# First tokens loaded ahead of the modulation weights, low parts of h fused, and one pair of heads loaded later: an adaLN transformer block on one core

## Chip, cores, metric

One Trainium2 chip, one NeuronCore. The metric is the device time of one execution in microseconds, median over runs. The engines are named as in the profile: PE (TensorE, with PEld for its weight loads), DVE (VectorE), ACT (ScalarE), POOL (GpSimd) and SP (SyncE, which in this kernel issues all the DMAs of before).

## What is computed

All is float32, with S = 2048 tokens, D = 512, 32 heads of 16, and a hidden width of 1792:

```
mod = silu(c) @ w_mod                    # 6 vectors of 512: sa, ca, ga, sb, cb, gb
h = layernorm(x) * (1 + ca) + sa
x = x + ga * (softmax_attention(h @ wqkv) @ wo)
h = layernorm(x) * (1 + cb) + sb
out = x + gb * (mish(h @ w1 + b1) @ w2)
```

## The kernel before

Matmuls get their precision from splitting: each operand is rounded to fp32r ("hi", suffix `_h`, `wh`, `qh`) and the rest is kept as a second fp32r tensor ("lo", `_l`, `wl`, `ql`). A product is three matmuls, hi·hi, hi·lo and lo·hi (`mm3`). `hi_copy` makes the first (L94 on ACT, L96 on DVE, L98 on POOL), `lo_sub` the second (L101).

The schedule is manual: every engine executes its instructions in the order in which the program emits them. The program has three stages.

1. **The prologue.** It loads x in 16 tiles of 128 tokens (`load_x`), the first two modulation vectors' weights (`wma`, 1 MB each) and slices of wqkv (`slice_load`), normalises the tokens and writes h and its low part, transposed, for four blocks of 512 tokens (`tb` 0 to 3). Per block: statistics on DVE and a few small POOL instructions (`stats_tb`), the normalisation in place on ACT (`apply_tb`, L385), transposes on PE into PSUM (L427 for the first block, L435 after), then `tr_tb`: ACT writes h_h (L440), DVE writes the unrounded value hf (L441), and DVE or POOL subtracts to give h_l (`LOV` names the k that DVE takes; L101). The first k and q products (L132 on `ring`) go in two parts: those that need only h_h early, those that need h_l late. Before that come the modulation vectors: 8 matmuls against `wma` (L449), two ACT copies (L453), 8 small matmuls that turn rows into columns (L455), and two DVE writes into `modc` (L463, L464); h_h needs both vectors. silu(c) is one ACT instruction and three of DVE (L361 to L364), on c loaded as a column of 512 single elements.
2. **The main loop.** `step(t)` for t from -20 to 511. It computes the row maxima of the scores (L553 and L539 with DVE reductions L555 and L541), the scores (L588), exponentials on ACT (L591), the products with v (L606), and beside them all remaining projections and the MLP as queued units. Hooks `at(h, f)` run f at half step h, so a step t has the hooks 2t and 2t+1; this is how every DMA of the loop gets its place in SP's queue. Heads are worked in pairs: `load_pair(pp)` is two loads of q rows (L313) and two of k rows (L322). Pair 3 is first read at t = 4, so at h = 8.
3. **The tail**, the MLP of the last block.

In SP's queue around the start of the loop: `load_pair(2)` at h = -22, `load_pair(3)` at -8, the four stores of the first maxima into q (`qa<-mt`, L577) at -6, `load_v(0)` (`vg`, L526) at -3, then the later modulation weights (`wm`, L700, by `mod_load`).

`free_banks` goes through the program at the end and drops the dependencies between two instructions of different engines on the ring of PSUM banks if they touch different banks and share no other tensor that one of them writes.

Of the kernel before, what the change touches and what calls it, by code (L numbers as in the profile page):

```python
# [18 lines left out]
def adaln_block(ctx: ExitStack, tc: tile.TileContext, x, wqkv, wo, w1, b1, w2, c, w_mod, out):  # L19
# [21 lines left out]
    LOV = ((1,), (), (1, 3), (1, 3))  # L41
# [10 lines left out]
    nc.scalar.preload_act_table_set("natural_log_exp_and_others")  # L52
# [22 lines left out]
    sel = cst.tile([P, 1], F32, name="sel")  # L75
    nc.gpsimd.memset(sel, 0.0)
    for k in range(DK):
        nc.gpsimd.memset(sel[32 * k:32 * k + 1, :], 1.0)
# [89 lines left out]
    def free_banks():  # L168
# [3 lines left out]
        for i in nc.cur_bb.bb.instructions:  # L172
            banks, names, made = set(), set(), set()
            for a in (*i.outs, *i.ins):
                v = getattr(a, "bass_ap", None)
                if v is not None and v.tensor.name != ring_t.tensor.name:
                    names.add(v.tensor.name)
                    if any(a is w for w in i.outs):
                        made.add(v.tensor.name)
# [149 lines left out]
    with ExitStack() as es:  # L329
        lp = es.enter_context(tc.tile_pool(name="lp", bufs=1))  # L330
        cc = lp.tile([P, DK], F32, name="cc")
        nc.sync.dma_start(cc, c.rearrange("o (k p) -> p (o k)", p=P))
# [7 lines left out]
        wma = [lp.tile([P, DK, D], F32, name=f"wma{i}") for i in range(2)]  # L340
# [13 lines left out]
        nc.gpsimd.memset(zer, 0.0)  # L354
        for i in range(NR):
            nc.gpsimd.memset(qa[i].bitcast(F32), 0.0)
        for i in range(2):
            nc.gpsimd.memset(ka[i].bitcast(F32), 1.0)

        e = lp.tile([P, DK], F32, name="sil_e")  # L360
# [3 lines left out]
        nc.vector.tensor_mul(sil, cc, e)  # L364

# [21 lines left out]
        def first_norm():  # L387

            mv = lp.tile([P, 4, 2], F32, tag="ln_mv4", name="ln_mv4", bufs=2)
            rs = lp.tile([P, 4, 4], F32, tag="ln_rs4", name="ln_rs4", bufs=3)  # L390
            for h in range(2):
                two = slice(2 * h, 2 * h + 2)
                for i in range(2 * h, 2 * h + 2):
                    st_ = lp.tile([P, 6], F32, tag="ln_st", name="ln_st", bufs=4)
                    nc.vector.bn_stats(out=st_, in_=xts[i])
                    nc.vector.bn_aggr(out=mv[:, i, :], in_=st_)
                nc.gpsimd.tensor_scalar(rs[:, 0, two], mv[:, two, 1], 1.0, EPS, op0=ALU.mult, op1=ALU.add)
                nc.gpsimd.tensor_scalar(rs[:, 3, two], mv[:, two, 0], -1.0, 0.0, op0=ALU.mult, op1=ALU.add)
                nc.gpsimd.tensor_tensor(rs[:, 1, two], rs[:, 0, two], nhalf.to_broadcast([P, 2]), op=ALU.pow)
                nc.gpsimd.tensor_mul(rs[:, 2, two], rs[:, 3, two], rs[:, 1, two])  # L400
                if h == 0:
                    hi_k = split_hi(1, 0)
            return rs, hi_k

        def split_hi(kind, i, eng="p"):
# [4 lines left out]
        def split_lo(kind, i, hi):  # L410
            lo = lp.tile([P, DK, P], F32R, tag="wl", name="wl", bufs=2)
            lo_sub("p", lo, slices[kind, i], hi)
            slices[kind, i] = (hi, lo)

        def first_apply(rs, i, eng):
            xt = xts[i]
            if eng == "a":
                nc.scalar.activation(xt, xt, AF.Identity, scale=rs[:, 1, i:i + 1], bias=rs[:, 2, i:i + 1])
            else:
                nc.vector.tensor_scalar(xt, xt, rs[:, 1, i:i + 1], rs[:, 2, i:i + 1], op0=ALU.mult, op1=ALU.add)  # L420

        def first_tr():
            pts = [bank(("ring", "ms", "ring", "acc")[k]) for k in range(DK)]
            for ii in ((0,), (1,), (2, 3)):
                for k in range(DK):
                    for i in ii:
                        nc.tensor.transpose(pts[k][:, i * P:(i + 1) * P], xts[i][:, k * P:(k + 1) * P], ident)  # L427
            return pts

        def tr_tb(tb, ks=range(DK), pts=None):  # L430
            for k in ks:
# [9 lines left out]
                nc.vector.tensor_scalar(hf, pt, modc[:, 1, k:k + 1], modc[:, 0, k:k + 1], op0=ALU.mult, op1=ALU.add)  # L441
                lo_sub("v" if k in LOV[tb] else "p", h_l[:, k, s], hf, h_h[:, k, s])

        rs, hi_k = first_norm()
        pr, pm = [], bank()[:, :2 * DK].rearrange("p (i k) -> p i k", k=DK)
        for i in range(2):
            pr.append(ring())
            for k in range(DK):
                nc.tensor.matmul(pr[i][32 * k:32 * k + 32, :], sil[:, k:k + 1].to_broadcast([P, 32]), wma[i][:, k, :],  # L449
                                 start=True, stop=True)  # L450
        for i in range(2):
            row = lp.tile([P, D], F32, tag="hf", name="row", bufs=6)
            nc.scalar.copy(row, pr[i])  # L453
            for k in range(DK):
# [1095 lines left out]
```

## Time and profile before

| | us |
|---|---|
| median of 3 runs | 1692.54 (1691.68 to 1693.66) |
| the profiled execution, its own time | 1691.02 |
| its span | 1689.2 |
| granted TensorE clock | 1.00 |

The profile page gives busy time by engine, the span in 40 slices, the DMA queues, the chain of work that ended last, and the costliest groups. The timeline gives instructions in order of time: start, duration, engine, line, operation, output<-inputs, shapes, count, and in brackets the idle time before and what ended it. Successive instructions of a line are merged (x4). "SPq" is SP issuing a DMA; its duration is that of the issue, not of the transfer. In the windows view the columns are PE, PEld, DVE, ACT and POOL busy us with counts, the granted clock, the busy share of the DMA engines and GB/s.

### The profile page before, as it was taken

What the parts mean: (1) busy time and instruction counts of PE and PEld (TensorE: products, weight loads), DVE (VectorE), ACT (ScalarE), POOL (GpSimd) and SP (SyncE); (2) the same over time, 40 slices, a digit from 0 to 9 for tenths busy, and PEclk for the clock granted to TensorE, in tenths of its full rate; (3) what the DMA queues carried; (4) which work ended last, traced back from release to release, by engine and by line L of the source; (5) the groups of instructions that cost most, each with busy time, mean ns of one, the idle gap of its engine ahead of it and who ended that gap; (6) DMA issues with size and microseconds to landing.
All of it is one profiled execution on the core that took longest, in us unless ns stands there. A gap on an engine that the chain in (4) does not pass through costs nothing.

```text
span 1689.2 us, 33772 instructions
## 1 busy us (share of the span) xinstructions
PE 1667.3 (99%) x12418; PEld 921.5 (55%) x12418; DVE 1441.5 (85%) x2369; ACT 1355.1 (80%) x2612; POOL 821.1 (49%) x843
## 2 busy tenths in 40 slices
PE   7999999999999999999999999999999999999999
PEld 5755655555444455555555455555555455555687
DVE  8898888888989988888889888888889888883377
ACT  6257777777778998888888998888888998889674
POOL 7555224655313564556323564556323565555442
PEclk9999999999999999999999999999999999999999
DMA  7877556777755443434355434534354533533261
GB/s 248 269 244 199 147 150 185 218 223 216 231 142 146 110 94 98 117 88 129 84 137 152 115 77 93 139 77 127 87 144 122 130 94 77 144 107 132 75 230 63
DMA packets 115406, 238.98 MB, mean 141 GB/s; under 512 B 24928, under 2 KB 50544, under 8 KB 109288
## 3 DMA queue, kind: packets, MB, share of 16 engines
q1 hardware_dynamic: 115240, 236.82, 49.9%
q8 instruction: 98, 1.61, 0.4%
q14 instruction: 68, 0.56, 0.1%
HBM read 180.48 MB, written 51.45 MB: 137 GB/s over the span
## 4 chain that ended last, share of the span: by engine, by line
PE 91%; DVE 3%; ACT 3%; DMA 2%; POOL 1%; issue 1%; SPq 0%; ACTq 0%; DVEq 0%; POOLq 0%
PE bk L606 29%; PE ring L588 22%; PE ring L539 20%; PE bk L139 11%; PE bk L132 3%; PE ring L1219 2%; PE ring L132 2%; DVE mx L541 2%; ACT pr L591 1%; PE ring L553 0%; DMA qa<-mt 0%; DMA xt<-in_A_x 0%; PE ring L922 0%; DMA kscr<-qh 0%; PE ring L568 0%
## 5 line engine op out<-in xcount | busy, mean ns | idle before, releaser
L541 DVE TENSOR_REDUCE mx<-ring 128x1 f32<-128x512 f32 x1968 | 1223.1, 682 | 150.0 <-PE ring L539 136.4
L591 ACT ACTIVATE pr<-ring 128x512 f32<-128x512 f32 x2048 | 1078.4, 603 | 207.1 <-PE bk L139 124.7
L539 PE MATMUL ring<-ka,qa 64*128 64x512 f32 x1968 | 817.9, 429 | 1.4 <-ACT pr L591 1.1
L588 PE MATMUL ring<-qa,ka 64*128 64x512 f32 x2048 | 759.1, 402 | 3.4 <-ACT pr L591 1.9
L606 PE MATMUL bk<-pr,vg 128*32 128x512 f32 x4096 | 545.1, 604 | 0.0
L539 PEld LDWEIGHTS ring<-ka,qa 64*128 64x128 f32 x1968 | 350.5, 184 | 326.2 <-DVE mx L541 251.3
L588 PEld LDWEIGHTS ring<-qa,ka 64*128 64x128 f32 x2048 | 373.7, 184 | 194.7 <-DVE mx L541 111.4
L139 PE MATMUL bk<-h,w 64*128 64x512 f32 (+1 forms) x1080 | 278.1, 390 | 0.0
L139 PE MATMUL bk<-w,a_h 64*128 64x512 f32 x632 | 210.9, 413 | 0.0
L139 PEld LDWEIGHTS bk<-h,w 64*128 64x128 f32 x1080 | 178.5, 184 | 9.3 <-ACT pr L591 1.5
L606 PEld LDWEIGHTS bk<-pr,vg 128*32 128x32 f32 x4096 | 81.2, 108 | 135.4 <-issue 126.0
L139 PE MATMUL bk<-w,a_l 64*128 64x512 f32 x316 | 124.0, 392 | 0.0
L139 PEld LDWEIGHTS bk<-w,a_h 64*128 64x128 f32 x632 | 106.8, 184 | 4.3 <-ACT hb L800 1.0
L978 POOL TENSOR_TENSOR y<-yd,y 128x512 f32<-128x512 f32 x44 | 56.9, 1293 | 89.0 <-ACT yd L977 79.7
L812 POOL TENSOR_SCALAR qq<-ee 128x512 f32<-128x512 f32 x25 | 15.5, 619 | 169.6 <-ACT ee L806 169.6
L828 POOL TENSOR_TENSOR qq<-qq,rr 128x512 f32<-128x512 f32 x42 | 54.1, 1289 | 85.9 <-ACT rr L822 85.9
L814 POOL TENSOR_TENSOR hb<-hb,ee 128x512 f32<-128x512 f32 x42 | 54.1, 1288 | 79.6 <-DVE ee L810 77.7
L139 PE MATMUL bk<-w,o_hl 64*128 64x512 f32 x288 | 79.1, 405 | 0.0
L101 POOL TENSOR_TENSOR a_l<-hb,a_h 128x512 fp32r<-128x512 f32 x53 | 73.1, 1379 | 4.4
L98 POOL TENSOR_SCALAR qh<-qf 128x512 fp32r<-128x512 f32 x27 | 16.7, 619 | 90.8 <-ACT qf L262 69.4
L139 PEld LDWEIGHTS bk<-w,a_l 64*128 64x128 f32 x316 | 58.3, 185 | 3.4
L139 PE MATMUL bk<-h_h,wl 64*128 64x512 f32 x168 | 57.2, 420 | 0.2 <-ACT pr L591 0.2
(219 smaller groups left out, 1909.1 us busy)
## 6 DMA issues: line engine op xcount, KB each, us to landing
ka<-kscr SPq DMA_DIRECT2D x124, 384.0 KB
w<-w2scr SPq DMA_DIRECT2D x56, 512.0 KB
w<-w1scr SPq DMA_DIRECT2D x46, 512.0 KB
vg<-vscr SPq DMA_DIRECT2D x32, 552.0 KB
qa<-qscr SPq DMA_DIRECT2D x124, 100.0 KB
kscr<-qh SPq DMA_DIRECT2D x16, 512.0 KB
qscr<-qh SPq DMA_DIRECT2D x32, 256.0 KB
w2scr<-hl SPq DMA_DIRECT2D x14, 512.0 KB
```

The costliest lines, as they stand in the source:

```text
L101: (nc.gpsimd if eng == "p" else nc.vector).tensor_sub(lo, src, hi.bitcast(F32))
L132: nc.tensor.matmul(acc, l, r, start=start, stop=stop)
L139: i = nc.tensor.matmul(acc, l[64 * g:64 * g + 64], r[64 * g:64 * g + 64], start=start and not then, stop=bool(stop and then))
L539: nc.tensor.matmul(pm, qt[64 * s:64 * s + 64, qs * P:(qs + 1) * P], kt[64 * s:64 * s + 64, kb * TB:(kb + 1) * TB], start=True, stop=True)
L541: nc.vector.tensor_reduce(out=mxs[n][:, s, 4 * j + qs, kb:kb + 1], in_=pm, op=ALU.max, axis=AX.X)
L588: nc.tensor.matmul(p_, kt[64 * s:64 * s + 64, kc * P:(kc + 1) * P], qt[64 * s:64 * s + 64, :], start=True, stop=True)
L591: e = nc.scalar.activation(pr, p_, AF.Exp, scale=SCALE)
L606: nc.tensor.matmul(accs[n][32 * h:32 * h + 32, :], vgs[n][:, o:o + 32], pts.pop((t, h)), start=(kc == 0), stop=(kc == 15))
L814: (nc.vector if tail else nc.gpsimd).tensor_mul(hb, hb, ee)
L828: nc.gpsimd.tensor_mul(qq, qq, rr)
L978: nc.gpsimd.tensor_add(y[i], yd, y[i])
L1219: nc.tensor.matmul(po[i // 2][:, i % 2, :], l[:, s], w[:, r, :], start=(f == 0 and j == 0), stop=(f == FT - 1 and j == 2))
```

## The change

It touches the prologue and one hook.

- c comes as a row of four runs of 512 bytes, on ACT's DMA queue, ahead of ACT's table load, and a PE transpose makes it a column.
- The loads go x 0 to 3, `wma` 0 in four parts, the first k slice, `wma` 1 in four parts, the first q slice, and the rest as before.
- PE transposes the identity into a spare bank, 8 times before c's transpose, 26 times after it and 4 times after the modulation (`keep_busy`).
- The fills of `ka` move from POOL to ACT copies, those of `qa` 3 and 4 and of `zer` behind POOL's first normalisation; the `sel` tile is gone.
- Each modulation vector is 16 matmuls of 128 columns, in the order of the loads, with a DVE copy, a PE transpose and a DVE write into `modc`.
- Statistics of tokens 0 to 1023 go by pairs of tiles (`stats_two`). Those of tiles 4 to 7 now stand on DVE behind the write of the second vector and ahead of the first block's hf.
- In `tr_tb`, hf becomes pt·scale - h_h in one DVE instruction, and h_l = hf + shift: a DVE add with a pointer scalar for the k in `LOV`, else a POOL add with a broadcast column. `LOV[0]` is (2, 3) instead of (1,).
- The split of the first v slice comes between the normalisations of tiles 5 and 6, so on DVE ahead of the third block's statistics instead of behind them.
- `free_banks` tells the blocks of h_h apart.
- `load_pair(3)` is at h = -2 instead of -8.

```diff
-    LOV = ((1,), (), (1, 3), (1, 3))
+    LOV = ((2, 3), (), (1, 3), (1, 3))
...
-        cc = lp.tile([P, DK], F32, name="cc")
-        nc.sync.dma_start(cc, c.rearrange("o (k p) -> p (o k)", p=P))
+        crow = lp.tile([DK, P], F32, name="crow")
+        nc.scalar.dma_start(crow, c.rearrange("o (k p) -> (o k) p", p=P))
+        nc.scalar.preload_act_table_set("natural_log_exp_and_others")
...
-        for i in range(2):
-            nc.sync.dma_start(wma[i], w_mod[:, i * D:(i + 1) * D].rearrange("(k p) m -> p k m", p=P))
+        def load_mod(i):
+            for k in range(DK):
+                nc.sync.dma_start(wma[i][k], w_mod[k * P:(k + 1) * P, i * D:(i + 1) * D])
         for t in range(4):
             load_x(t)
+        load_mod(0)
         slice_load(1, 0, lp, lp)
+        load_mod(1)
         slice_load(0, 0, lp, lp)
...
+        keep_busy(8)
+        cc = ring()[:, :DK]
+        nc.tensor.transpose(cc, crow, ident[:DK, :DK])
+        keep_busy(26)
...
+        hi_copy("a", ka[0], ones.to_broadcast([P, S]))
...
+        def mod_sums(i, ks):
+            for k in ks:
+                for m in range(DK):
+                    nc.tensor.matmul(prs[i][32 * m:32 * m + 32, :P], sil[:, k:k + 1].to_broadcast([P, 32]),
+                                     wma[i][k][:, m * P:(m + 1) * P], start=(k == 0), stop=(k == DK - 1))
+        def mod_cols(i):
+            row = lp.tile([P, P], F32, name=f"row{i}")
+            nc.vector.tensor_copy(row, prs[i][:, :P])
+            nc.tensor.transpose(prs[i][:, P:2 * P], row, ident)
+            cols = prs[i][:, P:2 * P:32]
...
-                nc.vector.tensor_scalar(hf, pt, modc[:, 1, k:k + 1], modc[:, 0, k:k + 1], op0=ALU.mult, op1=ALU.add)
-                lo_sub("v" if k in LOV[tb] else "p", h_l[:, k, s], hf, h_h[:, k, s])
+                nc.vector.scalar_tensor_tensor(hf, pt, modc[:, 1, k:k + 1], h_h[:, k, s].bitcast(F32), op0=ALU.mult,
+                                               op1=ALU.subtract)
+                if k in LOV[tb]:
+                    nc.vector.tensor_scalar_add(h_l[:, k, s], hf, modc[:, 0, k:k + 1])
+                else:
+                    nc.gpsimd.tensor_add(h_l[:, k, s], hf, modc[:, 0, k:k + 1].to_broadcast([P, TB]))
...
+        for q in range(2):
+            stats_two(q)
+        first_apply(3, "p")
+        for t in (*(t.bitcast(F32) for t in qa[3:]), zer):
+            nc.gpsimd.memset(t, 0.0)
+        mod_sums(0, (0, 1))
+        first_apply(0)
+        first_tr(0)
+        mod_sums(0, (2,))
+        first_apply(1)
+        first_tr(1)
+        mod_sums(0, (3,))
+        first_apply(2)
+        first_tr(2)
+        first_tr(3)
+        mod_cols(0)
+        hi_k = split_hi(1, 0, "a")
+        hi_copy("a", ka[1], ones.to_broadcast([P, S]))
+        split_lo(1, 0, hi_k, "v")
+        mod_sums(1, range(DK))
+        mod_cols(1)
+        keep_busy(4)
+        hi_q = split_hi(0, 0, "p")
+        split_lo(0, 0, hi_q, "p")
+        for q in range(2, 4):
+            stats_two(q)
+        tr_tb(0, pts=pts)
+        for i in range(4, 8):
+            first_apply(i)
+            if i == 5:
+                slice_split(2, 0, eng="v")
...
             if tb + 2 < NB:
                 stats_tb(tb + 2)
-            if tb == 0:
-                slice_split(2, 0, eng="v")
...
-    for pp, h in ((2, -22), (3, -8)):
+    for pp, h in ((2, -22), (3, -2)):
         at(h, lambda pp=pp: load_pair(pp))
```

More of the change, by code (lines that the diff above doesn't have):

```diff
@@ L176, in free_banks @@
                 if v is not None and v.tensor.name != ring_t.tensor.name:
[L177 removed]
+                    part = v.offset % (DK * S) // TB if v.tensor.name == h_h.tensor.name else 0
+                    names.add((v.tensor.name, part))
                     if any(a is w for w in i.outs):
[L179 removed]
+                        made.add((v.tensor.name, part))
                 elif v is not None:
@@ L451, in adaln_block @@
[L451 to L454, printed above, removed]
-                nc.tensor.matmul(pm[:, i, k:k + 1], row[:, k * P:(k + 1) * P], sel, start=True, stop=True)
-        for i in range(2):
-            first_apply(rs, i, "a")
-        split_lo(1, 0, hi_k)
-        hi_q = split_hi(0, 0, "a")
-        split_lo(0, 0, hi_q)
-        first_apply(rs, 2, "a")
-        first_apply(rs, 3, "v")
```

88 lines of the change are left out of this document (35 added, 53 removed).

## The prediction

> **What bounds the kernel now.** I read the page first, for what the end hangs on.
>
> ```profile
> span 1689.2 us, 33772 instructions
> PE 1667.3 (99%) x12418; PEld 921.5 (55%) x12418; DVE 1441.5 (85%) x2369; ACT 1355.1 (80%) x2612; POOL 821.1 (49%) x843
> PE 91%; DVE 3%; ACT 3%; DMA 2%; POOL 1%; issue 1%; SPq 0%; ACTq 0%; DVEq 0%; POOLq 0%
> ```
>
> PE is 91% of the chain; the other engines' shares must lie where PE isn't yet, or not always, the limit. The change alters only the prologue and one hook, so I read the chain of waits over the first 125 us next.
>
> ```profile
> 15.12 1.48 DVE xt L420
> ...
> 51.07 1.86 PE bk L132 x14
> ...
> 92.58 7.33 DMA kscr<-qh
> ```
>
> Ahead of 51 us the chain goes through DVE, POOL, ACT and a DMA as often as through PE (the first row is a DVE step of the first block). Behind 51 us it is PE nearly without a break, so what the prologue gains the end should gain too. Two views price the prologue: the windows, for the DMA rate, and the timeline.
>
> ```profile
> 0.00:5.00 5.00, 0.00 (x0) 0.00 (x0) 1.88 (x3) 1.49 (x2) 4.17 (x24) 1.00 0.51 140
> 5.00:10.00 5.00, 0.79 (x4) 0.20 (x8) 4.29 (x4) 0.00 (x0) 3.72 (x3) 1.00 1.05 408
> 10.00:15.00 5.00, 5.00 (x27) 2.62 (x19) 2.95 (x8) 2.67 (x5) 3.01 (x9) 1.00 1.08 387
> 15.00:20.00 5.00, 4.79 (x24) 4.47 (x23) 4.75 (x12) 2.07 (x4) 2.72 (x3) 1.00 1.06 400
> ```
>
> ```profile
> 0.72 0.44 SPq L332 DMA_DIRECT2D cc<-in_c  x1
> 3.17 0.20 ACT L361 ACTIVATE sil_e<-cc 128x4 f32<-128x4 f32 x1 [1.18 <-DMA cc<-in_c]
> 9.21 3.64 PE L449 MATMUL ring<-wma,sil 128*32 128x512 f32 x16 [9.21 <-DVE sil L364]
> 9.79 0.69 DVE L395 BATCH_NORM_STATS2 ln_st<-xt 128x6 f32<-128x512 f32 x1 [0.64 <-DMA xt<-in_A_x]
> 16.52 0.15 DVE L463 TENSOR_SCALAR modc<-bk 128x4 f32<-128x4 f32 x1
> 16.66 0.68 DVE L374 BATCH_NORM_STATS2 ln_st<-xt 128x6 f32<-128x512 f32 x1
> 18.18 0.42 PE L427 MATMUL bk<-ident,xt 128*128 128x128 f32 x1
> 18.39 0.64 PE L427 MATMUL ring<-ident,xt 128*128 128x128 f32 x2
> 19.07 0.78 ACT L440 ACTIVATE h_h<-ring,modc 128x512 fp32r<-128x512 f32 x1 [2.93 <-PE ring L427]
> 19.88 0.81 DVE L441 TENSOR_SCALAR hf<-ring,modc 128x512 f32<-128x512 f32 x1
> ```
>
> The DMA engines are full from 5 to 20 us, and x stands in their queue behind 2.1 MB of modulation weights. The first h_h comes at 19.07, after PE's transposes; the modulation was ready at about 16.7. DVE goes from four tiles' statistics at 16.66 straight into hf at 19.88: 3.2 us for four tiles. The rest of the prologue:
>
> ```profile
> 23.50 0.68 DVE L374 BATCH_NORM_STATS2 ln_st<-xt 128x6 f32<-128x512 f32 x1
> 25.74 2.08 PE L132 MATMUL ring<-h_l,wh 128*128 128x512 f32 x8
> 26.70 1.21 DVE L101 TENSOR_TENSOR wl<-wr,wh 128x1024 fp32r<-128x1024 f32 x1
> 29.43 5.06 POOL L101 TENSOR_TENSOR h_l<-hf,h_h 128x512 fp32r<-128x512 f32 x4
> 29.68 2.93 ACT L385 ACTIVATE xt<-xt,ln_rs 128x512 f32<-128x512 f32 x4
> 34.00 0.60 PE L435 MATMUL ring<-ident,xt 128*128 128x128 f32 x4
> 34.79 1.18 PE L132 MATMUL ring<-h_l,wh 128*128 128x512 f32 x4
> 35.28 0.19 POOL L376 TENSOR_SCALAR ln_rs<-ln_mv 128x4 f32<-128x4 f32 x1 [0.79 <-DVE ln_mv L375]
> 36.79 0.20 POOL L379 TENSOR_TENSOR ln_rs<-ln_rs 128x4 f32<-128x4 f32 x1
> 43.92 0.81 DVE L441 TENSOR_SCALAR hf<-ring,modc 128x512 f32<-128x512 f32 x1 [1.91 <-ACT h_h L440]
> 45.48 1.16 DVE L101 TENSOR_TENSOR h_l<-hf,h_h 128x512 fp32r<-128x512 f32 x1
> 49.36 1.05 PE L132 MATMUL ring<-h_l,wh 128*128 128x512 f32 x2 [1.03 <-POOL h_l L101]
> ```
>
> PE has little slack, but neither have DVE and POOL: the second block's h_l is ready at 29.43 + 5.06 = 34.5, and PE reads its fourth part at about 34.79 + 3 x 0.23 = 35.5. Before 49.36 PE waits outright for h_l, 1.03 us.
>
> **The loads.** The windows give the bytes moved: 0.70 MB by 5 us, 2.74 by 10, 4.67 by 15. The first x tile ends at 2.36 MB (two weight blocks of 1.05 MB and 0.26 MB), so at 9.1; DVE, which waited for it, sees it at 9.79, a lag of 0.7. In the new order x 0 to 3 end at 1.05 MB, the second vector's weights at 3.41, tile 7 at 4.72 as before. With c off SP everything starts about 0.4 earlier (L332). So the last part of the second vector lands at 11.7 - 0.4 + 0.7 = 12.0 and tile 7 at 15.1 - 0.4 + 0.7 = 15.4. Six more issues on SP hide behind a full queue; uncovered they would cost SP about 0.5 each.
>
> **The modulation.** The 16 products of 128 columns of one vector are as many columns as its four products of 512 (3.64 us for both vectors), so 0.45 for the part that lands last. Then a DVE copy of 128 columns (estimate 0.3, under half of L441's 512), a transpose (0.42), the write (0.15) and three handovers (0.15 together, estimate): modc is ready at 13.5. By then, if PE's transposes aren't late (a rival below), the tokens are transposed, and h_h starts there instead of at 19.07. The ACT copies that fill ka (at most four times L440's 0.78) and the POOL fills lie under the wait for weights. The POOL fills and `sel` removed from the start, the freed L362 and the old row-to-column matmuls gain nothing by themselves: the landing sets the time.
>
> **DVE's chain.** It now runs: modc, statistics of tiles 4 to 7 (13.5 + 3.2 = 16.7; tile 7 at 15.4 + 0.8 doesn't bind), the first block's hf and adds, the v split, the third block's statistics. The fused hf waits for h_h; that costs nothing, since at 43.92 the old hf already started when ACT's h_h ended. Its own price is not shown. From 19.88 to 23.50 lie four old hf and one subtraction, so 0.72 each; L441's 0.81 is the upper end, a two-operand pass of 512 columns the lower (0.65, by 26.70's 1.21 for 1024). I keep 0.72. The adds that end h_l are priced from these groups by form:
>
> ```profile
> L704 POOL TENSOR_TENSOR wm<-wm,sil 128x1024 f32<-128x1024 f32 x8 | 15.1, 1893 | 15.9 <-DMA wm<-in_w_mod 8.9 <-PE bk L139 5.7 <-PE bk L606 1.2
> L96 DVE CAST a_h<-hb 128x512 fp32r<-128x512 f32 x3 | 1.3, 428 | 0.3
> ```
>
> L704 has a broadcast operand as the new POOL add has, and takes 1.89 for 1024 columns; half of that is 0.95, and with a fixed part (estimate 0.1) 1.04 for 512, against 1.27 for the old subtraction (5.06 for four). Ends: 0.95 and 1.27. A DVE add with a pointer scalar stands between the one-operand cast (0.43) and L420's 1.48, which ran beside POOL. I take 0.9: nearest to the old subtraction beside POOL (1.16), less the 0.25 or so by which the cast is shorter than a two-operand pass.
>
> From 16.7: four hf (2.9), two adds (1.8) and the v split (1.2) bring the third block's statistics to 22.6 instead of 23.50; here most of the first 3.2 us is eaten, because the v split now stands ahead. They end at 25.8, POOL's scale takes 1.7 (35.28 to 36.99), to 27.5, four POOL adds take 4.2, to 31.7. PE needed the fourth at 35.5: 3.7 earlier. The third block's tokens are applied at 27.5 + 2.9 = 30.4, for a transpose that ran at 34.3: 3.9 earlier. The other path, ACT and PE in the first block (tiles 6 and 7 have their scale at 16.7 + 1.4, estimated from POOL's 1.7 for four columns; ACT applies them, 0.73 each, behind the v split until 20.5; the late products follow the transposes at 21.2, against 25.74), gives 4.5. The smallest binds; I take 3.6. In the fourth block PE's wait at 49.36 shrinks by two DVE adds that are 0.25 shorter: 0.5. Sum: 4.1 less.
>
> **The hook.** Pair 3's four issues leave their place in front of the maxima's stores and stand between vg and wm:
>
> ```profile
> 88.84 2.49 SPq L313 DMA_DIRECT2D qa<-qscr  x2
> 91.37 1.11 SPq L322 DMA_DIRECT2D ka<-kscr  x2
> 100.58 0.33 SPq L526 DMA_DIRECT2D vg<-vscr  x1
> 101.88 0.49 PE L588 MATMUL ring<-qa,ka 64*128 64x512 f32 x1
> ```
>
> They are 3.6 us of SP. In front, the k store at 92.58 took 7.33 to land, behind theirs; it lands sooner. Behind them are now wm and some k stores, which had the same bytes ahead of them before. Pair 3 is read four steps after 101.88, some 12 us (1587 us of span left for 512 steps); issued at 100.9 to 104.5 and with the 7.33 of a loaded queue it lands by 112, just inside. I cost it at nothing, with ends of -0.5 (POOL's waits for stores) and +3 (its landing late by as much as SP's own 3.6).
>
> Against the profiled execution, 1691.02 (span 1689.2 and 1.8 around it), the sum gives 1686.9; it lay 1.5 under the median. Against the median of 1692.54: **1688.4**. Its own range, from the ends of the adds and 0.5 either way of the landing, is 1687.2 to 1689.9.
>
> **Rivals.** *A. The low parts stop binding.* If the DVE adds run at 0.43, the first block's DVE work ends 0.9 sooner, PE's own path (4.5) binds, and the fourth block gives 0.8: 5.3, so 1687.2. For it: the operand shape; against it: POOL is busy beside each add.
>
> *B. DVE gives it back.* At 1.48 an add the third block's statistics come 1.2 later, the shift is 2.4, and the fourth block gives nothing: 1690.1.
>
> *C. PE stays at half rate in front of the modulation.* In the trace the first block's transposes are 0.21 apart (18.18 to 18.39), later four fit in 0.60 (34.00), about 0.11 apart: PE doubles somewhere between. The new order puts 26 transposes behind c and 16 more before the second vector. At 0.21, from c's landing at 3.2: 9.0 for the 42, 1.8 for each vector, 1.3 for columns: modc at 17.2, 3.7 later, and the gain is gone but for 0.4: 1692.1. At 0.11 the work ahead of the second vector ends before 12. [...] The trace does not decide it: at 18.39 the slow pitch still holds, and real matmuls lie between that and 34.00.
>
> *D. Slower: c comes late on ACT's queue.* All of PE's work waits for c's transpose, and no row shows a DMA issued by ACT. If it takes the 7.33 that 92.58 shows for a loaded queue, c lands at 8.0 instead of 3.2, and at half rate modc comes at 22.0, 8.5 late: 1696.9. From c at 7.0 on it is slower by over 0.2%; at full rate only from about 13. Against it: 3.17 shows c landing 2 us after SP's issue, and four runs of 512 bytes are less than 512 single elements.
>
> *E. Pair 3 is late.* PE stalls at t = 4 by up to 3: 1691.4.
>
> **How the numbers follow.** 0.2% is 3.4 us, about what a measurement of this kernel can tell from no change; the border is 1689.15. Forecast 0.53, of which 0.46 lies under the border and 0.07 above. A 0.14 (faster); B 0.09, C 0.12 and E 0.04 (all three within 0.2%); D 0.08 (slower). So faster 0.46 + 0.14 = 0.60, same 0.07 + 0.09 + 0.12 + 0.04 = 0.32, slower 0.08. The range goes from 1686.4, below A by the hook's 0.5 and 0.3 of landing time, to 1693.0, which takes in B, C and E and leaves out D.
>
> **What would show it.** Right: the first statistics start near 4 us; modc is written near 13.5; h_h follows at once; hf starts at 16.7; the third block's statistics at 22.6; POOL's adds take about 1.04; the second block's late products come 3.6 earlier than 34.79; the chain's step at 51.07 comes 4 us earlier and the loop keeps this; PE shows no new wait at pair 3's first products. Wrong: transposes still 0.21 apart at 9 us (C); c's transpose after 6 us (D); DVE adds over 1.3 (B); a PE wait on `ka` or `qa` near 110 (E).

## The result, and the profile after

The changed kernel takes **1688.34 us** (median of 11 executions, 1687.72 to 1691.65), the kernel before beside it 1691.31 (11 executions, 1690.26 to 1694.25). The ratio is 0.9982, 95% interval 0.9974 to 0.9990: about 3 us faster. Predicted were 1688.4, and 4.1 us of gain from a base of 1692.54. The base was 1.2 too high and the gain 1.1 too large, so the time is closer than its working by luck. The gain is small, 0.18%, just under the 0.2% that the prediction took as the border of what can be told, but its interval is clear of no change.

The page of the profiled execution after (1688.32, so its span can stand for the median):

```profile
span 1686.5 us, 33920 instructions
PE 1670.4 (99%) x12491; PEld 924.4 (55%) x12491; DVE 1432.9 (85%) x2372; ACT 1357.4 (80%) x2612; POOL 812.5 (48%) x839
PE 92%; DVE 3%; ACT 2%; DMA 1%; issue 1%; POOL 0%; SPq 0%; ACTq 0%; DVEq 0%; POOLq 0%
```

The span is 2.7 shorter, the chain's DMA and POOL shares are smaller, and PE's busy time is 3.1 longer, though the fill alone (the transposes of the identity in front of and between the products) adds about 7.0 (1.97, 4.40 and 0.60) and some products run at a granted clock of 0.50 (23.3 to 26.7 us, from the windows). The timeline after, at the steps that the prediction named. A line has another number than before: L127 was L132, L456 L435, L384 L374, L583 L553, L618 L588; L467 and L465 are the new adds, L462 the fused hf.

```profile
0.71 0.55 ACTq L328 DMA_DIRECT2D crow<-in_c  x1
3.24 0.26 PE L367 MATMUL ring<-ident,crow 4*128 4x4 f32 x1
4.24 0.68 DVE L403 BATCH_NORM_STATS2 ln_st<-xt 128x6 f32<-128x512 f32 x1
8.51 0.27 PE L433 MATMUL bk<-ident,xt 128*128 128x128 f32 x1
8.62 0.27 PE L433 MATMUL ring<-ident,xt 128*128 128x128 f32 x1
12.00 0.42 PE L438 MATMUL ring<-wma,sil 128*32 128x128 f32 x8 [0.22 <-DMA wma<-in_w_mod]
13.41 0.42 PE L438 MATMUL ring<-wma,sil 128*32 128x128 f32 x8 [0.29 <-DMA wma<-in_w_mod]
14.61 0.16 DVE L447 TENSOR_SCALAR modc<-ring 128x4 f32<-128x4 f32 x1 [0.42 <-PE ring L444]
14.81 0.78 ACT L461 ACTIVATE h_h<-ring,modc 128x512 fp32r<-128x512 f32 x1 [1.77 <-DVE modc L447]
18.27 0.72 DVE L462 SCALAR_TENSOR_TENSOR hf<-ring,modc,h_h 128x512 f32<-128x512 f32 x1
20.34 0.78 DVE L465 TENSOR_SCALAR h_l<-hf,modc 128x512 fp32r<-128x512 f32 x1
21.44 0.33 PE L456 MATMUL ring<-ident,xt 128*128 128x128 f32 x1 [1.32 <-ACT xt L424]
22.67 3.24 PE L127 MATMUL ring<-h_l,wh 128*128 128x512 f32 x8
23.35 0.68 DVE L384 BATCH_NORM_STATS2 ln_st<-xt 128x6 f32<-128x512 f32 x1
28.40 4.03 POOL L467 TENSOR_TENSOR h_l<-hf,modc 128x512 fp32r<-128x512 f32 x4
33.24 1.21 PE L127 MATMUL ring<-h_l,wh 128*128 128x512 f32 x4
46.74 0.78 PE L127 MATMUL ring<-h_l,wh 128*128 128x512 f32 x2 [0.16 <-POOL h_l L467]
47.46 0.74 PE L583 MATMUL ring<-ka,qa 64*128 64x512 f32 x4
98.95 0.50 PE L618 MATMUL ring<-qa,ka 64*128 64x512 f32 x1
```

Read down, the lead over the kernel before is 4.3 at the first h_h (14.81 against 19.07), 3.1 at the start of the late products (22.67 against 25.74), only 1.55 at the second block's (33.24 against 34.79), 2.9 at the first max product (47.46; the row of before is below) and at step 0's score (98.95 against 101.88), and 2.7 at the end.

```profile
50.34 0.73 PE L553 MATMUL ring<-ka,qa 64*128 64x512 f32 x4
```

So of the 4.3 won at the modulation 2.7 were lost by 33 us, and the rest of the prologue gave 1.3 back. The windows after show the first loss:

```profile
5.00:10.00 5.00, 5.00 (x56) 4.08 (x58) 2.42 (x7) 2.84 (x4) 3.37 (x10) 1.00 0.99 353
10.00:15.00 5.00, 3.81 (x54) 2.15 (x50) 1.60 (x6) 2.61 (x3) 1.92 (x5) 1.00 1.08 373
15.00:20.00 5.00, 4.33 (x19) 3.13 (x18) 4.72 (x11) 4.38 (x7) 3.92 (x10) 1.00 1.06 373
20.00:22.00 2.00, 0.44 (x2) 0.14 (x1) 1.93 (x4) 2.00 (x3) 2.00 (x2) 1.00 1.05 385
22.00:24.00 2.00, 1.86 (x9) 1.57 (x10) 2.00 (x3) 1.53 (x3) 0.01 (x1) 0.82 1.11 359
24.00:26.00 2.00, 2.00 (x7) 1.51 (x6) 1.90 (x7) 0.64 (x2) 0.00 (x0) 0.50 1.06 168
26.00:28.00 2.00, 2.00 (x11) 1.45 (x9) 1.97 (x5) 1.73 (x3) 1.20 (x3) 0.82 0.87 262
```

From 20 to 22 PE is busy for 0.44 of 2 us: it waits for tiles 6 and 7 (the 1.32 at 21.44). A little later the granted clock goes to 0.50 for about 3.4 us, and the eight late products take 3.24 where they took 2.08.

### The profile page after: what moved, and what is told of

Its sections match the earlier page's. It is cut to its first block, busy times and chain, and to the rows that moved or that the text cites. A ratio compares the mean times of both kernels' runs of the same rounds, so it can differ in the third digit from the quotient of the medians.

```text
span 1686.5 us, 33920 instructions
## 1 busy us (share of the span) xinstructions
PE 1670.4 (99%) x12491; PEld 924.4 (55%) x12491; DVE 1432.9 (85%) x2372; ACT 1357.4 (80%) x2612; POOL 812.5 (48%) x839
## 4 chain that ended last, share of the span: by engine, by line
PE 92%; DVE 3%; ACT 2%; DMA 1%; issue 1%; POOL 0%; SPq 0%; ACTq 0%; DVEq 0%; POOLq 0%
PE bk L636 29%; PE ring L618 22%; PE ring L569 19%; PE bk L134 11%; PE bk L127 3%; PE ring L127 2%; PE ring L1249 2%; DVE mx L571 2%; ACT pr L621 1%; PE ring L583 1%; DMA qa<-mt 0%; PE ring L952 0%; PE ring L598 0%; DMA xt<-in_A_x 0%; PE ring L134 0%
## 5 line engine op out<-in xcount | busy, mean ns | idle before, releaser
L618 PE MATMUL ring<-qa,ka 64*128 64x512 f32 x2048 | 759.0, 402 | 3.2 <-ACT pr L621 2.0
L618 PEld LDWEIGHTS ring<-qa,ka 64*128 64x128 f32 x2048 | 373.6, 184 | 192.2 <-DVE mx L571 113.3
L842 POOL TENSOR_SCALAR qq<-ee 128x512 f32<-128x512 f32 x25 | 15.5, 620 | 169.3 <-ACT ee L836 169.3
L93 POOL TENSOR_SCALAR qh<-qf 128x512 fp32r<-128x512 f32 x27 | 16.7, 620 | 88.3 <-ACT qf L258 68.1
```

The costliest lines, as they stand in the source:

```text
L618: nc.tensor.matmul(p_, kt[64 * s:64 * s + 64, kc * P:(kc + 1) * P], qt[64 * s:64 * s + 64, :], start=True, stop=True)
```

## Experiments

"Marks" below are the first max product, step 0's first score and the span, in the profiled execution; the kernel before has 50.34, 101.88, 1689.2 and the kernel after 47.46, 98.95, 1686.5.

| kernel | median | ratio to before | marks |
|---|---|---|---|
| after | 1688.34 | 0.9982 (0.9974 to 0.9990) | 47.46, 98.95, 1686.5 |
| gap filled | 1689.66 | 0.9992 (0.9984 to 1.0001) | 47.04, 98.76, 1691.8 |
| v split back | 1688.85 | 0.9987 (0.9978 to 0.9995) | 46.42, 97.87, 1687.8 |
| old low parts | 1692.83 | 1.0006 (0.9997 to 1.0015) | 51.91, 103.36, 1691.0 |
| hook back | 1690.62 | 0.9996 (0.9987 to 1.0004) | 46.34, 100.65, 1690.3 |
| whole loads | 1688.25 | 0.9982 (0.9973 to 0.9991) | 47.78, 99.24, 1686.5 |
| no fill | 1689.47 | 0.9992 (0.9983 to 1.0001) | 45.38, 96.83, 1685.4 |
| before, hook moved | 1691.22 | 0.9997 (0.9989 to 1.0006) | 50.26, 101.76, 1689.6 |
| v split back, clock kept | 1688.47 | 0.9986 (0.9977 to 0.9995) | 46.22, 97.64, 1686.7 |
| before, fused low parts | 1691.21 | 1.0003 (0.9995 to 1.0012) | 49.92, 101.43, 1690.7 |
| c on SP | 1688.94 | 0.9980 (0.9963 to 0.9998) | 47.39, 98.86, 1686.1 |
| clock kept, four early w1 | 1708.13 | 1.0099 (1.0083 to 1.0114) | 46.36, 97.82, 1705.5 |
| clock kept, w1 loads earlier | 1687.28 | 0.9977 (0.9967 to 0.9986) | 46.06, 97.50, 1685.0 |

Four profiled executions lie more than 1 us off the median of their kernel: the filled gap's 3.9 above, hook back's 1.4 above, the fused low parts' 1.25 above, no fill's 2.3 below. Their marks are used for places, not for times.

The first marks need the same care. Hook back's kernel differs from the kernel after in one line behind the prologue, so its prologue is the same line for line. Yet its late products start at about the same time and take 2.11 instead of 3.24, and its first max product comes 1.1 earlier. In its profiled execution the clock fell at 16.2 us, not at 23.3, where it costs more. A difference of about 1 in the first mark between two kernels with one profile each is therefore not yet an effect of an edit. Hook back's window (PE's busy time, then the granted clock), and its PE:

```profile
16.00:18.00 2.00, 2.00 (x6) 0.55 1.08 366
```

```profile
22.83 2.11 PE L127 MATMUL ring<-h_l,wh 128*128 128x512 f32 x8
46.34 0.74 PE L583 MATMUL ring<-ka,qa 64*128 64x512 f32 x4
```

### Undoing the fused low parts

```diff
-    LOV = ((2, 3), (), (1, 3), (1, 3))
+    LOV = ((1,), (), (1, 3), (1, 3))
...
-                nc.vector.scalar_tensor_tensor(hf, pt, modc[:, 1, k:k + 1], h_h[:, k, s].bitcast(F32), ...)
+                nc.vector.tensor_scalar(hf, pt, modc[:, 1, k:k + 1], modc[:, 0, k:k + 1], op0=ALU.mult, op1=ALU.add)
+                lo_sub("v" if k in LOV[tb] else "p", h_l[:, k, s], hf, h_h[:, k, s])
```

> The changed kernel with the old low parts: hf unrounded on DVE, then a subtraction, LOV as before. If the fused form carries the gain behind the third block, POOL's four in the second block take 5.1 instead of 4.0 us, PE waits 1.0 us or more for h_l in front of the main loop again, and the first product comes 1 to 1.5 later than 47.46. If only the earlier start carries it, it stays within 0.3.

The ratio rises from 0.9982 to 1.0006, by some 4 us, and the first max product comes 4.45 later. PE's timeline with the old low parts, first block:

```profile
22.75 0.75 PE L127 MATMUL ring<-h_l,wh 128*128 128x512 f32 x2
24.52 0.79 PE L127 MATMUL ring<-h_l,wh 128*128 128x512 f32 x1 [1.03 <-POOL h_l L96]
26.74 2.50 PE L127 MATMUL ring<-h_l,wh 128*128 128x512 f32 x5 [1.42 <-POOL h_l L96]
```

and POOL's of the same kernel:

```profile
23.19 3.49 POOL L96 TENSOR_TENSOR h_l<-hf,h_h 128x512 fp32r<-128x512 f32 x2 [1.35 <-DVE hf L462]
...
30.51 5.08 POOL L96 TENSOR_TENSOR h_l<-hf,h_h 128x512 fp32r<-128x512 f32 x4
```

The expected price was 1 to 1.5; it is three times that. What was expected came: POOL's four subtractions of the last block take 5.08, and a wait of 1.04 in front of the loop is back. What was not expected is the first block. PE waits 2.5 there for two subtractions that take 1.7 each while DVE runs a subtraction of 1024 columns (itself 1.79 instead of 1.21). The clock falls at 23.3 as in the kernel after, just ahead of these waits, but it stays at 0.50 till about 30.1, twice as long. In the kernel after PE waits for none of the first block's low parts. The rest of the change without this part is no faster than the kernel before.

### The fused low parts alone

```diff
 (the kernel before, with)
-    LOV = ((1,), (), (1, 3), (1, 3))
+    LOV = ((2, 3), (), (1, 3), (1, 3))
 (and the new hf and adds in tr_tb)
```

> The kernel before with the fused low parts alone (hf as scale, minus h_h in one DVE instruction, the shift added on DVE for k 2 and 3 of the first block, else on POOL); loads, order and hook as before. In the new prologue the fusion was worth 4.5 (1692.8 without it against 1688.3). Theory: alone it gives 1 to 1.5, since the new prologue's first block puts the low parts of h ahead of everything else, while before's first block waits for its tokens: the wait of 1.03 in front of 49.36 shrinks to about 0.2, and the second block's four POOL operations take 1.04 instead of 1.27: 1689.6 to 1690.3 against 1691.3. Rival 1: the fusion is the whole gain, and the new order of loads gives nothing even with it: 1688.3. Rival 2: nothing, since the tokens' arrival sets the pace until 35 us: 1691.

Nothing measurable (1.0003, 0.9995 to 1.0012); the expected 1 to 1.5 is refuted, the second rival is right. The late products start at 25.58 against 25.74: in the old order of loads they wait for tokens (0.38 for xt at 25.06), not for h_l. A new PE wait of 1.13 for ACT's h_h, in front of 30.13, puts the second block's late products 0.9 behind those of the kernel before (35.73 against 34.79). The first max product is still 0.4 earlier: the wait in front of 49.36 has shrunk to 0.19.

### The fourth pair's hook, both ways

```diff
 (the kernel after, with)
-    for pp, h in ((2, -22), (3, -2)):
+    for pp, h in ((2, -22), (3, -8)):
 (and the kernel before, with the opposite edit)
```

> The changed kernel with pair 3's loads at h = -8 as before. Predicted: no difference beyond 0.5 us; POOL's wait for the k store (3.7 us in front of 100) comes back, the first product of the loop's step 0 stays 2.9 ahead of the kernel before. If the hook carries part of the gain, the shift at step 0 shrinks by 0.5 or more.

> The kernel before with nothing but the fourth pair's loads moved from half step -8 to -2. With the new prologue, putting them back at -8 cost 2.3 (1690.6 against 1688.3), by a wait of 2.8 of PE for the maxima's stores in front of step 0. The prediction had the move at nothing, with ends of -0.5 and +3. Theory: the wait appears only where the prologue is shorter, since before step 0 of the kernel before PE shows no wait for these stores: the time is that of the kernel before within 0.4 (1690.9). Rival: the move is worth something by itself, as POOL waited 3.7 for a k store that landed slowly behind the pair's loads: 1 to 2 lower, 1689 to 1690.

On the kernel before, the move gives nothing (0.9997), as the prediction had it. On the new prologue it is worth some 2.4: back at -8 the ratio is 0.9996. That refutes the expected absence of a difference beyond 0.5. The intervals of the two ratios overlap, but the wait that comes with it is plain. PE with the hook back:

```profile
100.65 0.46 PE L618 MATMUL ring<-qa,ka 64*128 64x512 f32 x1 [2.77 <-DMA qa<-mt]
```

and SP's queue in front of that:

```profile
88.93 1.92 SPq L309 DMA_DIRECT2D qa<-qscr  x2
90.90 1.01 SPq L318 DMA_DIRECT2D ka<-kscr  x2
...
93.74 2.94 SPq L607 DMA_DIRECT2D qa<-mt  x4
```

The stores of the first maxima are issued at 93.74 behind the pair's loads. Here PE wants them at 97.9; the kernel before issues them at 94.67 and wants them only at 101.88. The move has no price of its own; it takes away the next wait, and that appears only where PE comes 3 to 4 us earlier.

### The gap at 20 to 22 us

```diff
 (gap filled: after the first block's early products)
+            if tb == 0:
+                for _ in range(16):
+                    nc.tensor.transpose(prs[0][:, :P], ident, ident)
 (v split back: no slice_split between the applies of tiles 5 and 6; instead)
                 stats_tb(tb + 2)
+            if tb == 0:
+                slice_split(2, 0, eng="v")
```

> The changed kernel with 16 more transposes of the identity on PE, behind the first block's early products, where PE had waited from 19.9 to 22.1 us for tiles 6 and 7. Clock theory: the granted clock, which was 0.50 from 24 to 26 us, stays at 1.00; the eight late products take 2.1 us instead of 3.2, and the main loop's first product comes 1.0 to 1.5 earlier than 47.46. The predicted chain (DVE and POOL set the pace in the second block): the clock stays up too, but the first product stays within 0.3 of 47.46.

> The changed kernel with the split of the first v slice at its old place, behind tile 7 on ACT and behind the third block's statistics on DVE. Clock theory: tiles 6 and 7 are normalised 1 us earlier, PE's wait shrinks from 2.2 to about 1.2 us, the clock stays at 1.00, and the first product of the main loop comes 1.5 to 2.5 earlier than 47.46, more than with the fill alone, because the statistics are 1.2 earlier as well. Predicted chain: 1.2 earlier by the statistics alone, whatever the clock does.

With the v split back PE waits 0.23 instead of 1.32 for tile 6, and the first max product comes 1.0 earlier. That this is the split's doing isn't shown: hook back, with the split in place, comes 1.1 earlier too. The filled gap's is 0.4 earlier, between what the two expectations stand for. In both kernels the clock stays 1.00 from 20 us on, but it has fallen before. Windows of the filled gap, then of the v split back:

```profile
15.00:17.00 2.00, 1.74 (x5) 1.35 (x6) 1.20 (x4) 2.00 (x4) 1.40 (x4) 0.62 1.07 364
17.00:19.00 2.00, 2.00 (x6) 1.59 (x5) 1.48 (x4) 1.36 (x3) 0.74 (x2) 0.52 1.06 379
```

```profile
15.00:17.00 2.00, 1.79 (x5) 1.46 (x6) 1.13 (x4) 2.00 (x4) 1.41 (x4) 0.65 1.05 358
17.00:19.00 2.00, 2.00 (x6) 1.52 (x6) 1.83 (x5) 1.37 (x3) 0.78 (x3) 0.50 1.06 379
```

Here the fall, at 15.5, follows the waits between the second vector's parts, from 12 to 15.5, as it does in hook back at 16.2. At the end neither kernel is ahead of the kernel after. Where the lead of the v split back goes, its chain of waits tells: a store of w1's parts (7.94 from 77.53), a store of k (8.11 from 85.53), the first modulation weights (10.52 from 100.18), and a PE wait of 0.7 for them at 120.9.

### The loads: whole vectors, no fill, c on SP

```diff
 (whole loads)
-            for k in range(DK):
-                nc.sync.dma_start(wma[i][k], w_mod[k * P:(k + 1) * P, i * D:(i + 1) * D])
+            nc.sync.dma_start(wmw[i], w_mod[:, i * D:(i + 1) * D].rearrange("(k p) m -> p k m", p=P))
 (no fill: without keep_busy(8), keep_busy(26), keep_busy(4))
 (c on SP)
-        nc.scalar.dma_start(crow, c.rearrange("o (k p) -> (o k) p", p=P))
+        nc.sync.dma_start(crow, c.rearrange("o (k p) -> (o k) p", p=P))
```

> The kernel after, with each modulation vector loaded as one transfer of 1 MB again instead of four of 256 KB, in the new order. In the kernel after, the second vector's last part reached PE at about 13.4 us where 12.0 was predicted, and the DMA engines moved 353 GB/s from 5 to 10 us where the kernel before moved 408. Theory: the four short transfers cost rate; then the window from 5 to 10 us goes back towards 400 GB/s, the second vector lands near 12.3, its 16 products follow in 0.4 at once, modc is written near 13.6 (1.0 earlier than 14.6) and the time is 0.5 to 1 lower, about 1687.6. Rival: the rate has nothing to do with the size of the transfers (the tokens ahead of them, or writes beside them, set it); then the vector lands at 13.4 as before and all its products come behind that: modc at about 14.9 and the time equal or 0.3 higher, 1688.3 to 1688.7.

> The kernel after without the 38 transposes of the identity that only keep PE busy (8, 26 and 4). Theory: these transposes alone brought PE to full rate by 8 us; without them the first block's transposes run 0.21 apart instead of 0.11 and the products with the first vector at half rate, up to the second vector's landing; that part has to wait for the second vector until 12.0 anyway, so h_h comes at 15.2 to 16.5 instead of 14.8, the early products start at half rate, and the time is 0.5 to 2 higher: 1688.9 to 1690.3. [...]

> The kernel after with c's load back on SP's queue, ahead of the tokens. Two questions. The price of c on ACT's queue: everything behind it on SP starts 0.5 later, c itself lands as before (PE's c transpose waits for 8 fill transposes anyway, until 3.2). And the DMA rate: with the new prologue the engines move 353 to 371 GB/s from 5 to 10 us and 370 to 376 from 15 to 20, with the old one 404 to 408 and 400; neither the size of the transfers nor the fill did that. Theory: a second hardware queue in use costs the rate; then it is back at 400 here, the second vector's last part lands near 12.5 in spite of the later start, and the time is 0 to 0.7 lower. Rival: the queue has nothing to do with it, the rate stays at 360 to 375 and the time is 0 to 0.5 higher, 1688.3 to 1688.8.

From 5 to 10 us the DMA engines move 371 GB/s with whole loads, 367 without fill, 340 with c on SP, and about 374 from 15 to 20 in all three, as in the kernel after; the two kernels with the old order move 404 and 405, then 400 and 401. So none of the three, undone alone, brings the rate back. Two more things are on record. In the new order the engines are not full at first: from 4.0 to 5.5 us the kernel after has a DMA share of 0.66 and 236 GB/s, the kernel before 1.04 and 407. From 15 to 20 both are full (1.06), and the rates differ all the same (373 and 400). ACT's fills of ka, which now run beside these loads (3.61 to 5.50 and 11.15 to 13.04), were not taken out. The cause stays open. Whole loads and c on SP leave the time alone.

Without the fill the kernel is 1.1 slower in the median (the intervals overlap). Its transposes of the first block:

```profile
8.18 0.42 PE L431 MATMUL bk<-ident,xt 128*128 128x128 f32 x1
8.39 0.42 PE L431 MATMUL ring<-ident,xt 128*128 128x128 f32 x1
...
11.15 0.27 PE L431 MATMUL bk<-ident,xt 128*128 128x128 f32 x1
11.26 0.27 PE L431 MATMUL ring<-ident,xt 128*128 128x128 f32 x1
```

At 8.2 they are 0.21 apart, in the kernel after at 8.5 0.11, and nothing but transposes of the identity, and c's, ran there before 7.76. One group of 26 of them took 4.40, where 26 at 0.21 would be 5.5. So in the kernel after the transposes alone brought PE from 0.21 to 0.11 apart (three in 0.90 from 1.34, eight in 1.04 from 6.80). The granted clock in the windows does not show this half rate: it reads 1.00 at 8 to 10 us in both kernels.

The time is in the expected range, but the expected path to it, a later h_h, is not what the profiled execution shows: its first product of h_h starts at 15.01, in the kernel after at 15.64. This execution is the fastest to step 0, because the second vector is there when PE comes to it at 12.1, and because the clock does not fall in it. It has the same waits for tiles 6 and 7 as the kernel after, and the same busy share of 0.50 over the 3.4 us up to 22.0:

```profile
20.65 0.33 PE L454 MATMUL ring<-ident,xt 128*128 128x128 f32 x1 [1.32 <-ACT xt L422]
21.87 2.12 PE L127 MATMUL ring<-h_l,wh 128*128 128x512 f32 x8
```

So such a stretch does not always bring a fall. The other executions without fill, nine of eleven between 1688.95 and 1693.16, were not profiled; that the clock falls in them is only argued.

### Keeping the clock, and the queue behind it

```diff
 (v split back, and)
-        mod_sums(1, range(DK))
-        mod_cols(1)
-        keep_busy(4)
+        for k in range(DK):
+            mod_sums(1, (k,))
+            keep_busy(2)
+        mod_cols(1)
+        keep_busy(9)
```

> The kernel after with (1) the v split back behind the first block, so that PE's wait of 1.3 for tile 6 goes, and (2) two transposes of the identity after each quarter of the second vector's products and nine instead of four behind them, so that PE isn't idle for about 40% of the time from 12 to 15.6 us. In all runs with the new prologue the granted clock falls to 0.50 for about 3.4 us, either from 15.6 or from 23.4 on, after a stretch of idle PE. Theory: the fall comes from the idle stretch; with it filled the clock stays 1.00 to 30 us, the first block's products take 1.2 to 1.7 less than in the run with the v split alone, and the first max product comes at 45 to 45.8 against 46.4 there and 47.5 in the kernel after. By the time at the end this gives 1686.5 to 1687.5, if the DMA queue in front of step 0 (full from 60 to 95 us in these runs) doesn't take it back. Rival: that queue and the modulation's weights behind it bind already, as the runs with the gap filled and with the v split back show (ahead by 0.4 to 1 at the first max product, not ahead at the end): 1688.3 to 1689, with PE waiting for wm near 120. If the clock falls all the same, the idle time was not its cause.

The clock shows 1.00 in every window to 32 us, and so it does in the two kernels built on this one. Seven of the eight profiled executions of the new prologue without this fill show a fall to 0.50, at 15.5 to 16.2 or at 23.1 to 23.3; none of the three with it does. The idle stretch is thus the likely cause, but not the whole of it: no fill had a share of 0.50 without a fall, and four early w1, below, one of 0.56 from 18.6 to 22.0. What else decides stays open.

```profile
22.23 2.11 PE L127 MATMUL ring<-h_l,wh 128*128 128x512 f32 x8
```

The gain is small where it was looked for, 46.22 against 46.42, below the range expected, for two reasons. PE waits for tiles 6 and 7 behind the fall in both (0.23 and 0.38 with the v split back, 0.62 and 0.38 here), so tile 6 sets the pace: its transposes start at 21.20 and 21.00. And the fill has a price: with two transposes behind each quarter PE comes to the last quarter at 13.91 instead of 12.97, and h_h starts 0.9 later (15.31 against 14.37). At the end the rival is right. PE's waits from 90 to 130 us:

```profile
PE ring L571 <- ACT pr L623: 0.9, 1, 0.9
PE bk L134 <- ACT pr L623: 0.7, 2, 0.5
PE ring L127 <- POOL wm L738: 0.6, 1, 0.6
```

Two kernels test whether the DMA queue in front of step 0 makes them.

```diff
 (four early w1)
-    EARLY = 6
+    EARLY = 4
 (w1 loads earlier: the last block's load_k moves behind three of the early loads)
+    for i in range(3):
+        early_load(i)
+    for pp in range(2):
+        load_k(pp, NB - 1)
```

> The kernel with the v split back and the clock kept (1688.5), with four instead of six of the early preparations of w1 (each loads 0.26 MB and stores 0.52 MB in front of step 0); the two others move into the main loop's chain of preparations. In the kernel with the clock kept PE is 1.3 ahead of the kernel after at step 0 and has lost it again by step 8: its chain goes through a store of w1's parts (9 us), a store of k and the first modulation weights (10 us), with the DMA engines full from 60 to 95 us. Theory: that queue is the new bound; with 1.5 MB less in it (some 4 us of the engines at 350 GB/s) the waits behind step 0 (0.9 for exponentials and 0.6 for the modulation's weights) go and the end comes 1 to 1.6 earlier, 1687.0 to 1687.5. Rival: these waits come from the order of SP's and POOL's work rather than from the bytes, or the two preparations delay the MLP later: 1688.5 or more.

> The kernel with the v split back and the clock kept (1688.5), with three of the early w1 loads issued on SP ahead of the last block's k rows instead of behind them, and nothing else moved. In that kernel the DMA engines are half idle from 45 to 60 us (share 0.48 to 0.60) and POOL does nothing from 54 to 65.5, where it waits for these loads, which stand on SP behind k rows that wait for their store; from 65 to 95 us the engines are full. With two preparations taken out of that queue the waits behind step 0 went (first score at 97.8, PE without a gap from 110 to 130), but the rest of the loop was then worse by 20. Theory: the queue in front of step 0 is the bound, and the loads there come 4 us earlier, so POOL's first split starts at about 61 instead of 65.5, the stores of w1's parts come 3 to 4 us earlier, the waits of 0.9 for exponentials and 0.6 for the modulation's weights shrink or go, and the time is 0.5 to 1.5 lower: 1687.0 to 1688.0, the first that is below the kernel after. Rival: the engines are full by the bytes behind 65 us whatever POOL's start (16 MB from 65 to 125), the waits stay, and the time is 1688.4 to 1688.8.

With two preparations fewer the waits for exponentials and for wm are gone and step 0's region has no new one, but the loop behind it is worse by 20: PE waits 6.7 at once for POOL's a_h and is idle for 8 us from 1500 to 1600. How the two later preparations lead to that was not followed. With the loads only moved, POOL's first split starts earlier. POOL with the clock kept, then with the loads earlier:

```profile
65.52 0.63 POOL L93 TENSOR_SCALAR ep<-ep 128x512 fp32r<-128x512 f32 x1 [11.43 <-DMA ep<-in_B_w]
```

```profile
60.71 0.63 POOL L93 TENSOR_SCALAR ep<-ep 128x512 fp32r<-128x512 f32 x1 [6.78 <-DMA ep<-in_B_w]
```

The two waits are gone here too, and the time is 1687.28 (10 executions, 1686.41 to 1688.55), the lowest of all. Its ratio, 0.9977 (0.9967 to 0.9986), overlaps that of the kernel after; against the kernel with the clock kept it is 1.2 less. That difference is one of medians, and the two intervals overlap. With the waits that went, it points to the queue in front of step 0 as the next bound.

## Why the prediction was right, step by step

**The loads: wrong by 1.4.** The second vector's last part was to land at 12.0; its products start at 13.41. The prediction took the old windows' bytes for the new order (408 and 387 GB/s); the new order gets 353 and 373. By half-microsecond windows the 3.41 MB ahead of it had moved at 12.0, where the prediction had 11.3, and PE saw the last part 1.4 later, where 0.7 was taken: half of the lateness is the rate, half this lag. In other executions of the same loads the products start at 12.97 (v split back), 13.03 (gap filled) and 13.59 (hook back), so the step was wrong by 1.0 to 1.6. By itself this moves everything behind it by 1.3.

**The modulation: right.** From the last landing to modc 1.4, predicted 1.5; modc at 14.8 instead of 13.5, and h_h at once behind it. Its first premise held: first statistics at 4.24, c's transpose at 3.24, so rival D did not come.

**DVE's and POOL's chain: the prices right or too high, and not binding.** hf starts 18.27 (16.7), late by the landing. hf takes 0.72, as taken. The first block's two DVE adds take 0.78 and 0.49 instead of 0.9 each, so the third block's statistics, 23.35, are only 0.75 late on 22.6. POOL's adds take 1.04, as worked out (four in 4.03), and end at 32.43, 0.8 before PE reads the first. B is refuted (one add of six took 1.36).

**"The smallest binds": the failed step.** The prediction had PE's own path as the one with most to spare, 4.5 earlier. It is the one that bound, and it was 3.1 earlier at 22.67 and 1.55 at 33.24. The first part of what is missing is the landing once more: the late products were to start at 21.2 and start 1.5 later. The rest is a mechanism that the prediction did not have: behind PE's wait for tiles 6 and 7 the clock falls to 0.50, the late products take 3.24 instead of 2.08, and 1.5 of the lead are gone by 28.3. The chain of DVE and POOL, which the prediction took as the smallest, ended ahead of PE. Rival A's mechanism, low parts that stop binding, came, but without the 4.5 that it counted on. Rival C's, PE at half rate, came too, but at 23 (granted clock 0.50) instead of ahead of the modulation, where the transposes were 0.11 apart (at 8.5), and behind idle time. The share that the clock has in this differs by execution: in hook back's the lead is 2.6 at the second block (32.15) and 4.0 at the first max product. The working has a slip here too: 35.5 less 31.7 is 3.8, not 3.7, and 3.6 was then taken without a reason.

**The last block: too small.** 0.5 was taken; PE's wait went from 1.03 to 0.16 and the lead grew by 1.3 in all; the rest is 0.2 in the third block and 0.3 in shorter last products (0.78 instead of 1.05).

**The hook: right in the sum, wrong in the reason.** It costs nothing, as taken, and E, the pair being late, did not come: no PE wait for ka or qa near 110. But the shift could not have been carried into the loop without it: at -8 a wait of 2.77 takes it back. Nothing in the prediction asked whether the maxima's stores would be in time for an earlier PE.

**The sum.** Predicted 3.6 + 0.5 + 0 = 4.1; found 1.55 + 1.3 + 0, about 2.9 at step 0 and 2.7 to 3 at the end. The loop kept the lead, as forecast. That 1688.4 came out so near is luck, since two misses of some 1.1 cancel. And the rule that what the prologue gains the end should gain too holds here only to about 3 us: with the clock kept PE is 4.2 ahead at step 0 (97.64 against 101.88), but the kernel gains 2.9. With the w1 loads earlier it is 4.4 ahead and gains 4.1 (1687.28 against 1691.34). The queue in front of step 0 is a bound that the prediction did not have. The order of the loads, the statistics by pairs and the moved fills were not undone one by one, so their own shares are not shown.

## What to carry to other kernels

Parts of a change that shorten one serial stretch are not additive: alone, the fused low parts and the hook were worth nothing, but the fused low parts undone took the whole gain, and the hook undone most of it (2.3 of 3.0). When a stage is to end 3 or 4 us earlier, list what the next stage needs at its new start (stores, loads, another engine's copies) and ask for each whether it would be there. A short wait of TensorE cost twice here, where the clock fell to 0.50 behind it (3.24 instead of 2.08 for eight products). Filling the waits kept the clock at 1.00, but showed no gain at the end until the loads in the next queue were moved (1688.47, then 1687.28). And two profiles of the same prologue differed by 1.1 us in a mark (47.46 and 46.34), and the clock fell at another place in them (23.3 and 16.2): look where it fell before a difference is put down to an edit.

## What the runs showed of the hardware

- The granted clock fell to 0.50 in eight of the profiled executions, each time after PE was only partly busy; the longest idle stretch in front of a fall was 1.9 us (the fused low parts alone). Seven falls lasted 3.4 us; with the old low parts, where PE went on waiting, it was 6.8. Adding the one-microsecond windows over the 3.4 us in front of a fall, a stretch as long as the fall, gives a busy share of 0.50 (after, up to 23.3) and about 0.59 (the filled gap, the v split back, the hook back and the fused low parts, up to 15.5 to 16.5); busy ends are modelled, so these are rough. A low share did not always bring a fall: there was none behind 0.50 (no fill) and 0.56 (four early w1). Kernels with much the same idle stretches had the fall at 23.1 to 23.3 (four of them) or at 15.5 to 16.5 (four others, one of these with the old order of loads), and two with the same prologue, after and hook back, differ in it.
- A POOL add of 512 columns with a broadcast operand takes 1.04 us (one of ten 1.22), a POOL subtraction of two full operands 1.27. It took 1.74 while DVE ran a subtraction of 1024 columns (old low parts), and 1.27 beside DVE's other work.
- A DVE add with a pointer scalar takes 0.49 to 1.36 for the same 512 columns.
- With the tokens ahead of the modulation weights the DMA engines moved 331 to 376 GB/s between 5 and 20 us (windows of 5 us), with the weights ahead 387 to 408. This was not expected, and its cause is open; from 4.0 to 5.5 us the engines were not full in the new order (share 0.66, against 1.04).
- PE ran the first block's transposes at half rate at 8.2 us (0.21 apart; 0.11 at 11.15; no fill), and the granted clock of the windows read 1.00 at both.
